# Leaving the masked quarter of each attention chunk out of two matrix products: 64x64 tiles in a one-core kernel of lightning attention and a tanh-shrink MLP

## The chip, the cores and the metric

The kernel runs on one core of a Trainium2 chip. The metric is the device time of one execution in microseconds (us); lower is better. Before the change three runs gave 674.28, 672.62 and 675.01 us, so the median is 674.28 us.

## The reference, cut to what matters

Two steps follow one another. The first is a causal linear attention with decay: for each of 4 batches and 8 heads (sequence 768, head width 64) the sequence is taken in blocks of 64. A block's output is a part inside the block plus a part from a 64x64 state that is carried along.

```python
rel = pos[:, None] - pos[None, :]                      # block = 64
Dmask = np.where(rel >= 0, lam[:, None, None] ** rel[None, :, :], 0.0)
for b in range(nb):                                    # 12 blocks
    intra = np.einsum('bhic,bhjc->bhij', qb, kb) * Dmask[None]
    intra = np.einsum('bhij,bhjd->bhid', intra, vb)
    inter = np.einsum('bhid,bhde->bhie', qb * lam_pow[None], kv_state)
    out[:, :, sl] = intra + inter
    kv_state = lam_block[None, :, None, None] * kv_state \
             + np.einsum('bhsd,bhse->bhde', kb * rev_pow[None], vb)
```

The result, seen as `x` of shape (3072, 512), then goes through

```python
h = x @ w_in            # 512 x 2048
g = h - np.tanh(h)
return g @ w_out        # 2048 x 512
```

The two weight matrices arrive as 64-bit floating point numbers and are rounded to 32 bit inside the kernel. All products are float32.

## The kernel before, in words

**Groups and halves.** The kernel takes the sequence in chunks of 128 (not 64), which is allowed because the state recurrence can be cut anywhere: inside a chunk the 128x128 lower triangle of the decay mask takes the place of the 64x64 one. There are six groups, g = 0 to 5; a group is one chunk of all four batches, 512 tokens. Attention of a group runs in two halves, batches 0 and 1 (called p0 in the driver) and batches 2 and 3 (p1). The eight heads are four pairs p = 0 to 3 with j = 0, 1 inside a pair.

**Attention of one half.** `att_transpose` brings q and k into the form "head width on partitions" (on TensorE for g = 0 and 1; for later groups the blocks of 32x32 come by many small loads, line 143, and VectorE transposes them). `att_scores` computes for each batch the scores `sp` = keys times queries, 128x128 per head, into two PSUM banks (line 351), and VectorE multiplies a bank of 512 columns with `mask` into `ss` (line 355). `att_out` gathers the half's output in two PSUM banks `op`: first state times decayed queries (line 399, 64x64 tiles of TensorE), then v times `ss` (line 405, 128x64 tiles, all 128 keys and all 128 queries); ScalarE copies the banks to `xt` (line 409). `att_state` decays the keys (line 360), multiplies them with v into `kv` (line 373), lets VectorE multiply `state` with `lam_blk` (line 378) and add `kv` (line 379). `att_sums` makes four sums of `xt` for the second step.

**The second step.** Both matrix products run as a two-by-two scheme with seven products instead of eight (in parts twice nested); its sums of weights are made once, written to DRAM, and come back piece by piece as `wb` on GpSimd's queue. TensorE lines 457 and 541 make h, line 740 h of group 0, lines 632, 685 and 769 the product with w_out. The sums of g for them (lines 619, 656, 669 to 671, 690, 695 to 701) are VectorE's.

**Order.** A scheduler keeps each engine's instructions in the order in which they are written where they are tied, and may move others by its own model of times. The driver lays the attention of group g+1 between the product steps of group g: `p0[0]` and `p0[1]` (transposes, scores) inside `up`, `p0[2:]` (output, state) after `down(g, 2)`, then `p1[0]`, `p1[1]` and `p1[2:]` between the `down_twice` steps. So between a half's scores and its output there are always other products on TensorE; and on VectorE a half's state update stands in one queue with the sums of g. For group 1 the same pieces lie between the steps of `up_plain` (line 740) and before `down_first` (line 769), while the weights are still being loaded and rounded.

**PSUM and loads.** `sp`, `op` and `kv` take turns in four banks. k, v and q come in "natural" form (sequence on partitions) by one load per batch and tensor on SyncE's queue (line 131), 256 KB each.

Of the kernel before, what the change touches and what calls it, by code (L numbers as in the profile page):

```python
# [9 lines left out]
F32 = mybir.dt.float32  # L10
# [5 lines left out]
AF = mybir.ActivationFunctionType  # L16
AL = mybir.AluOpType

BLK = 128
GB = 2  # L20
# [4 lines left out]
def kernel(  # L25
# [61 lines left out]
    dram = ctx.enter_context(tc.tile_pool(name="dram", bufs=1, space=bass.MemoryType.DRAM))  # L87


    ident = const.tile([128, 128], F32)  # L90
    make_identity(nc, ident)
    lam_all = const.tile([128, H], F32)
    nc.scalar.dma_start(out=lam_all, in_=bass.AP(tensor=lam.tensor, offset=lam.offset, ap=[[0, 128], [1, H]]))

    mask = const.tile([128, 2, NP, BLK], F32)
    for j in range(2):
        for p in range(NP):
            h = 2 * p + j
            nc.vector.tensor_tensor_scan(out=mask[:, j, p, :], data0=lam_all[:, h:h + 1].to_broadcast([128, BLK]),
                                         data1=ident, initial=0.0, op0=AL.mult, op1=AL.add)  # L100

    fwd = const.tile([128, NP, BLK], F32)

# [8 lines left out]
            m *= 2  # L112


    bwd = mask.rearrange("s j p i -> s p j i")[:, :, :, BLK - 1:BLK].to_broadcast([128, NP, 2, D])

    lam_blk = fwd[:, :, BLK - 1:BLK][:, None, :, :].to_broadcast([128, 2, NP, D])

    def tied(yes, op):
        return tc.keep_in_program_order(op) if yes else op  # L120


    raw, late = {}, {}
# [3 lines left out]
    def load_natural(g, b, names):  # L127
        for name, src, bufs in (("q", q, 2), ("k", k, 3), ("v", v, 4)):
            if name in names:
                x = (qpool if name == "q" else io).tile([128, H, D], F32, name=f"{name}_nat", tag=name, bufs=bufs)  # L130
                op = nc.sync.dma_start(out=x, in_=src[b, :, ts(g, BLK), :].rearrange("h s d -> s h d"))
                tc.keep_in_program_order(op)
                raw[g, b][name] = x

    def load_blocks(g, b, names):
# [86 lines left out]
    def weights(n):  # L222

        while ready["done"] < min(n, len(blocks)):
            at_ = ready["done"]
            load_weights(at_ + WAHEAD)
            kind, n_, m = blocks[at_]
            if kind == "out" and m == 0:
                pair[n_] = pair_tiles(n_)
            w = w1[n_][:, m] if kind == "in" else pair[n_][m][:, 0:2]  # L230
            if at_ in wraw:
                round_block(w, wraw.pop(at_), at_ < 2 * KI)
            else:
                load_block(nc.gpsimd, w, kind, n_, m)
            ready["done"] += 1
# [16 lines left out]
    def sums_out(kt):  # L252
        x, y = pair[kt]
        b11, b12, b21, b22, t1, t2, t4, t3 = (t[:, i] for t, n in ((x, 2), (y, 6)) for i in range(n))
        nc.vector.tensor_tensor(t1, b12, b11, op=AL.subtract)
        nc.vector.tensor_tensor(t2, b22, t1, op=AL.subtract)
        nc.vector.tensor_tensor(t3, b22, b12, op=AL.subtract)
        nc.vector.tensor_tensor(t4, b21, t2, op=AL.subtract)
        f = factors[:].rearrange("x p k c -> p x k c")
        nc.gpsimd.dma_start(out=f[:, 0:1, kt, :], in_=x[:, 0:1, :])  # L260
        nc.gpsimd.dma_start(out=f[:, 1:NX, kt, :], in_=y[:, 0:2, :])

        for n, j in ((1, 0),) if kt % 2 == 0 else ((2, 0), (3, 1)):
            nc.gpsimd.dma_start(out=fine[:, SUB.index(n), :, kt // 2, :].rearrange("n p c -> p n c"),
                                in_=y[:, 1:6, ts(j, 128)])
# [31 lines left out]
    def bank(name, tag, bufs):  # L297
        return psum.tile([128, 512], F32, name=name, tag=tag, bufs=bufs)
# [18 lines left out]
    state = const.tile([128, B, NP, D], F32)  # L317


    tr, sc, kdec, xt = {}, {}, {}, {}  # L320
# [23 lines left out]
    def att_scores(g, bs):  # L344
        for b in bs:
            qt, kt, _ = tr[g, b]

            sp = [bank("sp", "att", 4).rearrange("s (p i) -> s p i", p=NP) for _ in range(2)]
            for p in range(NP):
                for j in range(2):  # L350
                    tied(g == 0, nc.tensor.matmul(out=sp[j][:, p, :], lhsT=kt[ts(j, 64), p, :],  # L351
                                                  rhs=qt[ts(j, 64), p, :], start=True, stop=True))
            ss = work.tile([128, 2, NP, BLK], F32, name="ss", tag="ss")
            for j in range(2):
                tied(g == 0, nc.vector.tensor_tensor(ss[:, j], sp[j], mask[:, j], op=AL.mult))  # L355
            sc[g, b] = ss

    def att_decay(g, b):
        kp = raw[g, b]["k"].rearrange("s (p j) d -> s p j d", j=2)
        tied(g != 1, nc.vector.tensor_tensor(kp, kp, bwd, op=AL.mult))  # L360

    def att_state(g, bs):
        if g == NG - 1:
            return

        kv = bank("kv", "att", 4).rearrange("d (b p e) -> d b p e", b=2, p=NP)
        for n, b in enumerate(bs):
            kd, vn = raw[g, b]["k"], raw[g, b]["v"]
            if g > 0:
                att_decay(g, b)  # L370
            for p in range(NP):
                for j in range(2):
                    tied(g == 0, nc.tensor.matmul(out=kv[ts(j, 64), n, p, :], lhsT=kd[:, 2 * p + j, :],
                                                  rhs=vn[:, 2 * p + j, :], start=n == 0 and p == 0, stop=True,
                                                  skip_group_check=True))
        st = state[:, bs[0]:bs[0] + 2]
        if g > 0:
            nc.vector.tensor_tensor(st, st, lam_blk, op=AL.mult)
            nc.vector.tensor_tensor(st, st, kv, op=AL.add)
        else:  # L380
            tied(True, nc.scalar.activation(st, kv, AF.Copy))

    def att_out(g, bs):
        half = bs[0] // 2
        xt[g, half] = xpool.tile([128, KI, HB], F32, name=f"xt{half}", tag=f"xt{half}")

        ops = [bank("op", "att", 4).rearrange("d (p b s) -> d p b s", p=2, b=2) for _ in range(2)]

        def dst(n, p, j):
            return ops[p // 2][ts(j if p < 2 else 1 - j, 64), p % 2, n, :]  # L390


        if g > 0:
            for n, b in enumerate(bs):
                for p in (0, 1):
                    for j in range(2):
                        r = ts(j, 64)
                        for pp in (p, p + 2):
                            nc.tensor.matmul(out=dst(n, pp, j), lhsT=state[r, b, pp, :], rhs=tr[g, b][2][r, pp, :],  # L399
                                             start=n == 0 and p == 0, stop=False, skip_group_check=True)  # L400
        for n, b in enumerate(bs):
            ss, vn = sc.pop((g, b)), raw[g, b]["v"]
            for p in range(NP):
                for j in range(2):
                    tied(g == 0, nc.tensor.matmul(out=dst(n, p, j), lhsT=vn[:, 2 * p + j, :], rhs=ss[:, j, p, :],  # L405
                                                  start=g == 0 and n == 0 and p % 2 == 0,
                                                  stop=n == 1 and p % 2 == 1, skip_group_check=True))
        for x in range(2):
            tied(g == 0, nc.scalar.activation(
                xt[g, half][:, 2 * x:2 * x + 2, :].rearrange("d p (b s) -> d p b s", b=2), ops[x], AF.Copy))  # L410
# [9 lines left out]
        xt[g] = dict(B11=b11, B21=b21, B22=b22, T1=tt[:, 0], T2=tt[:, 1], T3=b12, T4=tt[:, 2])  # L420

    def attention(g):
        pieces = [[(fn, g, bs) for fn in (att_transpose, att_scores, att_out, att_state)] for bs in ((0, 1), (2, 3))]
        pieces[1].append((att_sums, g, None))
        return pieces

# [368 lines left out]
    def run(pieces):  # L795
        for fn, *args in pieces:
            fn(*args)


    for b in (0, 1):  # L800
# [31 lines left out]
    p0, p1 = attention(1)  # L832
    load(B + 2)
    turns = [(1, 11, 1, ()), (1, 21, 1, ()), (1, 12, 1, ()), (1, 22, 1, ()), (2, 11, 2, p0[0:1]), (2, 21, 2, p0[1:2]),
             (3, 11, 1, ()), (3, 21, 1, p0[2:4]), (2, 12, 1, ()), (2, 22, 1, p1[0:1]), (3, 12, 1, p1[1:2]),
             (3, 22, 1, ())]
    for u, c, n, more in turns:
        every(up_plain(u, (c,)))
# [8 lines left out]
            if u == 2:  # L847
                sums_in(0)
    sums_out(0)
    run(p1[2:4])  # L850
    weights(NU * KI + 6)
    run(p1[4:])
    for kt in range(KH):
        down_first(kt, (1, 2))
        if kt + 1 < KH:
# [99 lines left out]
```

## Time and profile before

| what | value |
|---|---|
| runs | 674.28, 672.62, 675.01 us (median 674.28) |
| profiled execution: span, first to last instruction | 670.7 us |
| around the span, by the median | 3.6 us |
| clock granted to TensorE | 1.00 in every stage |
| TensorE busy, share of the span | 654.7 us, 98% |
| VectorE busy | 477.8 us, 71% |
| ScalarE busy | 215.2 us, 32% |
| GpSimd busy | 199.0 us, 30% |
| `sp` products, line 351 (records, mean) | 384 records, 279 ns |
| `op` from state, line 399 | 320 records, 276 ns |
| `op` from `ss`, line 405 | 384 records, 275 ns |
| `kv`, line 373 | 320 records, 223 ns |

The profiled execution's time is known only as its span; what lies around it is taken as the 3.6 us by which the median is longer. A float32 product leaves two records in the trace, so 192 products of line 351 are 384 records. The mean of a record is its duration from fetch to end and says little on the pace, since records overlap; the pace is read from the distance of their starts. Of the 670.7 us some 57 at the start are ruled by the loading of w_in (the DMA engines are busy 96% of them), the next 76 by a chain of rounding, sums and DRAM round trips, and from 133 us on TensorE is busy nearly without a gap.

### The profile page before, as it was taken

The numbers are of one execution on the slowest core, as the hardware profiler recorded it, in microseconds if no ns is written. First come the engines' busy times: TensorE is split into PE (matmuls) and PEld (weight loads), VectorE is DVE, ScalarE is ACT, GpSimd is POOL, SyncE is SP. The second block draws the span as 40 slices with busy tenths as digits, with TensorE's granted clock in tenths as the row PEclk, the third lists the DMA queues.
The fourth block names the chain that finished last, engine by engine and source line by source line (L and its number), as shares of the span: only waits on it lengthen the run. The fifth ranks groups of instructions, "written<-read, shape, count | busy, mean of one in ns | idle before, by whom it ended". The sixth has DMA issues, their size and how long they took to land.

```text
span 670.7 us, 13240 instructions
## 1 busy us (share of the span) xinstructions
PE 654.7 (98%) x4992; PEld 594.8 (89%) x4992; DVE 477.8 (71%) x869; ACT 215.2 (32%) x413; POOL 199.0 (30%) x346
## 2 busy tenths in 40 slices
PE   8899989999999999999999999999999999999998
PEld 7688878788888899988999988899988899988897
DVE  4467988966877985379896378888358978357753
ACT  4778924512321112342112243112333112334110
POOL 0001444773022435101345200254300244400251
DMA  9999964999235979544698741698830676610395
GB/s 210 225 207 256 303 206 146 321 264 264 56 81 127 261 220 290 129 85 107 170 293 250 190 79 45 156 291 245 247 72 5 159 244 205 223 46 1 110 297 174
DMA packets 161007, 121.76 MB, mean 182 GB/s; under 512 B 133872, under 2 KB 135024, under 8 KB 160944
## 3 DMA queue, kind: packets, MB, share of 16 engines
q0 software_dynamic: 27264, 89.41, 41.4%
q1 hardware_dynamic: 133536, 31.50, 24.1%
q8 instruction: 40, 0.66, 0.4%
q14 instruction: 23, 0.19, 0.1%
q10 hardware_dynamic: 144, 0.00, 0.0%
HBM read 100.67 MB, written 20.19 MB: 180 GB/s over the span
## 4 chain that ended last, share of the span: by engine, by line
PE 69%; issue 11%; DMA 7%; DVE 5%; ACT 3%; POOL 3%; SPq 2%; POOLq 0%; DVEq 0%; ACTq 0%
PE y L457 12%; PE y L685 12%; PE zw L685 9%; PE z L457 8%; PE y L541 4%; PE w L632 4%; PE y L632 4%; PE acc L769 3%; DMA raw<-in_moe_w_in_dram 3%; PE sp L351 2%; PE z L541 2%; PE op L405 2%; SPq L210 1%; DMA fine<-f 1%; PE op L399 1%
## 5 line engine op out<-in xcount | busy, mean ns | idle before, releaser
L597 POOL DMA_DIRECT2D wb<-fine x168 | 90.5, 539 | 138.2 <-PE y L685 61.8
L465 ACT ACTIVATE th<-g 128x512 f32<-128x512 f32 x76 | 47.6, 630 | 99.2 <-DVE g L470 34.2
L688 ACT ACTIVATE q<-y 128x128 f32<-128x128 f32 x96 | 26.6, 277 | 149.5 <-PE y L685 148.5
L600 POOL DMA_DIRECT2D wb<-factors x44 | 23.8, 542 | 170.1 <-PE y L632 127.8
L457 PE MATMUL y<-xt,w 128*128 128x256 f32 x320 | 73.5, 380 | 0.0
L457 PEld LDWEIGHTS y<-xt,w 128*128 128x128 f32 x320 | 59.9, 190 | 8.5 <-ACT g L545 0.9
L466 DVE TENSOR_TENSOR g<-g,th 128x512 f32<-128x512 f32 x76 | 52.1, 688 | 21.1 <-ACT th L465 21.0
L685 PE MATMUL y<-wb,g 128*128 128x128 f32 x456 | 60.6, 278 | 0.0
L740 PE MATMUL h<-xt,w 128*128 128x256 f32 x256 | 58.1, 383 | 2.1 <-DVE w L295 2.1
L740 PEld LDWEIGHTS h<-xt,w 128*128 128x128 f32 x256 | 47.7, 190 | 10.0 <-DVE w L295 2.6
L685 PEld LDWEIGHTS y<-wb,g 128*128 128x128 f32 x456 | 55.1, 192 | 1.3 <-issue 0.3
L685 PE MATMUL zw<-wb,g 128*128 128x128 f32 x304 | 40.3, 275 | 0.1
L457 PE MATMUL z<-tt,ws 128*128 128x256 f32 x160 | 38.1, 381 | 0.0
L457 PE MATMUL y<-tt,ws 128*128 128x256 f32 x160 | 37.8, 379 | 0.0
L457 PE MATMUL z<-xt,ws 128*128 128x256 f32 x160 | 37.8, 379 | 0.0
L685 PEld LDWEIGHTS zw<-wb,g 128*128 128x128 f32 x304 | 37.0, 192 | 0.3 <-DVE g L690 0.3
L632 PE MATMUL w<-wb,g 128*128 128x256 f32 x160 | 35.8, 382 | 0.0
L769 PE MATMUL acc<-wt,g 128*128 128x256 f32 x144 | 33.2, 381 | 2.4 <-DVE g L775 2.4
L632 PE MATMUL y<-wb,g 128*128 128x256 f32 x160 | 35.3, 379 | 0.0
L355 DVE TENSOR_TENSOR ss<-sp,mask 128x512 f32<-128x512 f32 x48 | 31.0, 682 | 5.8 <-PE sp L351 5.8
L457 PEld LDWEIGHTS z<-xt,ws 128*128 128x128 f32 x160 | 30.4, 190 | 4.1
L632 PEld LDWEIGHTS y<-wb,g 128*128 128x128 f32 x160 | 30.4, 190 | 4.1
(179 smaller groups left out, 1291.2 us busy)
## 6 DMA issues: line engine op xcount, KB each, us to landing
wb<-fine POOLq DMA_DIRECT2D x168, 256.0 KB, 4.0
wb<-factors POOLq DMA_DIRECT2D x44, 256.0 KB, 4.1
raw<-in_moe_w_out_dram POOLq DMA_DIRECT2D x16, 512.0 KB, 5.4
v_nat<-in_v_dram SPq DMA_DIRECT2D x24, 256.0 KB, 4.9
wb<-fine_in POOLq DMA_DIRECT2D x24, 256.0 KB, 4.4
k_nat<-in_k_dram SPq DMA_DIRECT2D x20, 256.0 KB, 4.9
raw<-in_moe_w_in_dram SPq DMA_DIRECT2D x8, 512.0 KB, 6.2
raw<-in_moe_w_in_dram SPq DMA_DIRECT2D x16, 256.0 KB, 6.2
```

The source lines that it names most:

```text
L355: tied(g == 0, nc.vector.tensor_tensor(ss[:, j], sp[j], mask[:, j], op=AL.mult))
L457: nc.tensor.matmul(out=t[:, m, :], lhsT=wt[:, kt, ts(m, 128)], rhs=x[:, kt, :], start=first and m == 0 and kt == 0, stop=kt == 1, skip_gro ...
L465: nc.scalar.activation(th, src, AF.Tanh)
L466: nc.vector.tensor_tensor(dst(c), src, th, op=AL.subtract)
L541: nc.tensor.matmul(out=dst[:, ts(u, 128)], lhsT=a, rhs=b, start=x in (1, 2, 5) and u == 0, stop=True, skip_group_check=True)
L597: nc.gpsimd.dma_start(out=t.rearrange("p m c -> p (m c)"), in_=fine[TWICE.index(n_), SUB.index(x_)].rearrange("p u c -> p (u c)"))
L600: nc.gpsimd.dma_start(out=t, in_=factors[XAT[FACT[n_][1]]][:, 2 * x_:2 * x_ + 2, :])
L632: nc.tensor.matmul(out=t[:, m, :], lhsT=a[:, u, kt, ts(m, 128)], rhs=wb[:, kt, :], start=first and u == 0 and m == 0 and kt == 0, stop=u = ...
L685: nc.tensor.matmul(out=dst, lhsT=a[:, u, :], rhs=wb[:, ts(u, 128)], start=x in (1, 2) and u == 0, stop=u == NU - 1, skip_group_check=True)
L688: nc.scalar.activation(keep, dst, AF.Copy)
L740: tied(u == 0, nc.tensor.matmul(out=hm[c][:, m, :], lhsT=w1[u][:, i, a, ts(m, 128)], rhs=xt[0, t][:, i, :], start=m == 0 and i == 0, stop= ...
L769: nc.tensor.matmul(out=acc[n][:, r, :], lhsT=a[:, ts(r, 128)], rhs=b, start=kt == 0 and r == 0, stop=kt == KH - 1, skip_group_check=True)
```

## The change

Of a chunk's 128x128 scores (key by query) the quarter with keys 64 to 127 and queries 0 to 63 is masked to zero as a whole. The change leaves that quarter out of both products with 64-row blocks, and packs the other three.

- `mask` keeps three quarters per head: 6 blocks of 64 columns per j instead of 4 of 128. It is made from the whole mask by two further VectorE copies and an addition; `ident` gets 64 more columns.
- k and v are loaded so that heads 4 to 7 have their sequence halves exchanged (keys 64 to 127 on partitions 0 to 63). Each such load is three DMAs instead of one: heads 0 to 3 whole, heads 4 to 7 in two halves of partitions.
- `att_scores`: per head one product of keys 0 to 63 with all 128 queries, and one of keys 64 to 127 with queries 64 to 127, both in 64x64 tiles; per half 32 products instead of 16. The multiplication with the mask takes 384 columns instead of 512.
- `att_out`: for queries 64 to 127 one product per head with all keys (128x64 tile, 64 columns); for queries 0 to 63 one with keys 0 to 63 (64x64 tile, 64 columns). The `kv` products now stand between these two sets, and the keys are decayed before.
- The multiplication of `state` with `lam_blk` moves into `att_out`, is written for group 5 as well, and every product of the last set waits for it by an explicit dependency.
- `att_state` remains for group 0 alone; a half has three pieces instead of four.

```diff
-    mask = const.tile([128, 2, NP, BLK], F32)
+    nc.vector.tensor_copy(wide[:, 128:192], wide[:, 0:64])
+    mask = const.tile([128, 2, 6, HALF], F32)
...
+    nc.vector.tensor_copy(mask[:, :, 2:6, :], whole[:, :, :, HALF:BLK])
+    nc.vector.tensor_tensor(mask[:, :, 0:2, :], whole[:, :, 0:2, 0:HALF], whole[:, :, 2:4, 0:HALF], op=AL.add)
...
-                op = nc.sync.dma_start(out=x, in_=src[b, :, ts(g, BLK), :].rearrange("h s d -> s h d"))
-                tc.keep_in_program_order(op)
+                rows = src[b, :, ts(g, BLK), :].rearrange("h s d -> s h d")
+                if name == "q":
+                    parts = [(x, rows)]
+                else:
+                    parts = [(x[:, 0:4], rows[:, 0:4])] + [(x[ts(1 - t, HALF), 4:8], rows[ts(t, HALF), 4:8])
+                                                           for t in range(2)]
+                for to, of in parts:
+                    tc.keep_in_program_order(nc.sync.dma_start(out=to, in_=of))
...
-            for p in range(NP):
+            for p in (0, 2, 1, 3):
+                x, r = p % 2, p // 2
                 for j in range(2):
-                    tied(g == 0, nc.tensor.matmul(out=sp[j][:, p, :], lhsT=kt[ts(j, 64), p, :],
-                                                  rhs=qt[ts(j, 64), p, :], start=True, stop=True))
+                    kj, qj = kt[ts(j, 64), p, :], qt[ts(j, 64), p, :]
+                    k0, k1 = (kj[:, ts(t if r == 0 or g >= GB else 1 - t, HALF)] for t in range(2))
+                    tied(g == 0, nc.tensor.matmul(out=sp[j][ts(r, HALF), x:3 + p:2 + p - x, :], lhsT=k0,
+                                                  rhs=qj.rearrange("d (t i) -> d t i", t=2), start=True, stop=True))
+                    tied(g == 0, nc.tensor.matmul(out=sp[j][ts(1 - r, HALF), 2 + p, :], lhsT=k1,
+                                                  rhs=qj[:, HALF:BLK], start=True, stop=True))
...
+            decayed = nc.vector.tensor_tensor(st, st, lam_blk, op=AL.mult)
+        for n, b in enumerate(bs):
+            ss, vn = sc[g, b], raw[g, b]["v"]
+            for p in range(NP):
+                for j in range(2):
+                    tied(g == 0, nc.tensor.matmul(out=dst(n, p, j)[:, HALF:BLK], lhsT=vn[:, 2 * p + j, :],
+                                                  rhs=ss[:, j, 2 + p, :], start=g == 0 and n == 0 and p % 2 == 0,
+                                                  stop=n == 1 and p % 2 == 1, skip_group_check=True))
+        kv = kv_products(g, bs) if 0 < g < NG - 1 else None
         for n, b in enumerate(bs):
             ss, vn = sc.pop((g, b)), raw[g, b]["v"]
-            for p in range(NP):
+            for x in range(2):
                 for j in range(2):
-                    tied(g == 0, nc.tensor.matmul(out=dst(n, p, j), lhsT=vn[:, 2 * p + j, :], rhs=ss[:, j, p, :],
-                                                  start=g == 0 and n == 0 and p % 2 == 0,
-                                                  stop=n == 1 and p % 2 == 1, skip_group_check=True))
+                    for p in (x, 2 + x):
+                        r = ts(p // 2, HALF)
+                        op = nc.tensor.matmul(out=dst(n, p, j)[:, 0:HALF], lhsT=vn[r, 2 * p + j, :],
+                                              rhs=ss[r, j, x, :], start=False, stop=n == 1 and x == 1,
+                                              skip_group_check=True)
+                        tied(g == 0, op)
+                        if decayed is not None:
+                            tc.add_manual_dep(op.ins, decayed.ins.name, mybir.DependencyInfo(
+                                mybir.DependencyClass.Sync, mybir.DependencyReason.DATA), reason="rows")
+        if kv is not None:
+            nc.vector.tensor_tensor(st, st, kv, op=AL.add)
```

In the changed kernel the products of line 351 are at lines 373 and 375, those of line 405 become lines 429 (queries 64 to 127) and 439 (queries 0 to 63), line 399 becomes 422, line 373 becomes 393, and the multiplication of the state, line 378, becomes line 424.

More of the change, by code (lines that the diff above doesn't have):

```diff
@@ L87 @@
     dram = ctx.enter_context(tc.tile_pool(name="dram", bufs=1, space=bass.MemoryType.DRAM))
-    ident = const.tile([128, 128], F32)
+    wide = const.tile([128, 192], F32, name="ident")
+    ident = wide[:, 0:128]
     make_identity(nc, ident)
@@ L93 @@
     nc.scalar.dma_start(out=lam_all, in_=bass.AP(tensor=lam.tensor, offset=lam.offset, ap=[[0, 128], [1, H]]))
-    mask = const.tile([128, 2, NP, BLK], F32)
+    HALF = BLK // 2
+    nc.vector.tensor_copy(wide[:, 128:192], wide[:, 0:64])
+    mask = const.tile([128, 2, 6, HALF], F32)
+    whole = xpool.tile([128, 3, 2, HB], F32, name="whole", tag="tt").rearrange("s a b c -> s (a b c)")[:, 0:2 * DM].rearrange(
+        "s (j p i) -> s j p i", j=2, p=NP)
     for j in range(2):
@@ L98 @@
             h = 2 * p + j
-            nc.vector.tensor_tensor_scan(out=mask[:, j, p, :], data0=lam_all[:, h:h + 1].to_broadcast([128, BLK]),
-                                         data1=ident, initial=0.0, op0=AL.mult, op1=AL.add)
+            nc.vector.tensor_tensor_scan(out=whole[:, j, p, :], data0=lam_all[:, h:h + 1].to_broadcast([128, BLK]),
+                                         data1=ident if p < 2 else wide[:, HALF:HALF + BLK], initial=0.0, op0=AL.mult,
+                                         op1=AL.add)
+    nc.vector.tensor_copy(mask[:, :, 2:6, :], whole[:, :, :, HALF:BLK])
+    nc.vector.tensor_tensor(mask[:, :, 0:2, :], whole[:, :, 0:2, 0:HALF], whole[:, :, 2:4, 0:HALF], op=AL.add)
     fwd = const.tile([128, NP, BLK], F32)
@@ L112, in powers @@
             m *= 2
-    bwd = mask.rearrange("s j p i -> s p j i")[:, :, :, BLK - 1:BLK].to_broadcast([128, NP, 2, D])
+    bwd = mask.rearrange("s j p i -> s p j i")[:, 2:6, :, HALF - 1:HALF].to_broadcast([128, NP, 2, D])
     lam_blk = fwd[:, :, BLK - 1:BLK][:, None, :, :].to_broadcast([128, 2, NP, D])
@@ L346, in att_scores @@
             qt, kt, _ = tr[g, b]
-            sp = [bank("sp", "att", 4).rearrange("s (p i) -> s p i", p=NP) for _ in range(2)]
-            for p in range(NP):
+            sp = [bank("sp", "att", 4)[:, 0:6 * HALF].rearrange("s (x i) -> s x i", x=6) for _ in range(2)]
+            for p in (0, 2, 1, 3):
+                x, r = p % 2, p // 2
                 for j in range(2):
-                    tied(g == 0, nc.tensor.matmul(out=sp[j][:, p, :], lhsT=kt[ts(j, 64), p, :],
-                                                  rhs=qt[ts(j, 64), p, :], start=True, stop=True))
-            ss = work.tile([128, 2, NP, BLK], F32, name="ss", tag="ss")
+                    kj, qj = kt[ts(j, 64), p, :], qt[ts(j, 64), p, :]
[4 more added lines that the diff above has]
+                                                  rhs=qj[:, HALF:BLK], start=True, stop=True))
+            ss = work.tile([128, 2, 6, HALF], F32, name="ss", tag="ss")
             for j in range(2):
@@ L360, in att_decay, with kv_products @@
         tied(g != 1, nc.vector.tensor_tensor(kp, kp, bwd, op=AL.mult))
-    def att_state(g, bs):
-        if g == NG - 1:
-            return
+    def kv_products(g, bs):
         kv = bank("kv", "att", 4).rearrange("d (b p e) -> d b p e", b=2, p=NP)
@@ L368, in att_state @@
             kd, vn = raw[g, b]["k"], raw[g, b]["v"]
-            if g > 0:
-                att_decay(g, b)
             for p in range(NP):
@@ L375, in att_state @@
                                                   skip_group_check=True))
[L376 to L381, printed above, removed]
+        return kv
+    def att_state(g, bs):
+        kv = kv_products(g, bs)
+        tied(True, nc.scalar.activation(state[:, bs[0]:bs[0] + 2], kv, AF.Copy))
     def att_out(g, bs):
@@ L385, in att_out @@
         xt[g, half] = xpool.tile([128, KI, HB], F32, name=f"xt{half}", tag=f"xt{half}")
+        st = state[:, bs[0]:bs[0] + 2]
         ops = [bank("op", "att", 4).rearrange("d (p b s) -> d p b s", p=2, b=2) for _ in range(2)]
@@ L390, in dst @@
             return ops[p // 2][ts(j if p < 2 else 1 - j, 64), p % 2, n, :]
+        decayed = None
         if g > 0:
+            if g < NG - 1:
+                for b in bs:
+                    att_decay(g, b)
             for n, b in enumerate(bs):
@@ L422, in attention @@
     def attention(g):
-        pieces = [[(fn, g, bs) for fn in (att_transpose, att_scores, att_out, att_state)] for bs in ((0, 1), (2, 3))]
+        pieces = [[(fn, g, bs) for fn in (att_transpose, att_scores, att_out)] for bs in ((0, 1), (2, 3))]
         pieces[1].append((att_sums, g, None))
@@ L834 @@
     turns = [(1, 11, 1, ()), (1, 21, 1, ()), (1, 12, 1, ()), (1, 22, 1, ()), (2, 11, 2, p0[0:1]), (2, 21, 2, p0[1:2]),
-             (3, 11, 1, ()), (3, 21, 1, p0[2:4]), (2, 12, 1, ()), (2, 22, 1, p1[0:1]), (3, 12, 1, p1[1:2]),
+             (3, 11, 1, ()), (3, 21, 1, p0[2:]), (2, 12, 1, ()), (2, 22, 1, p1[0:1]), (3, 12, 1, p1[1:2]),
              (3, 22, 1, ())]
@@ L849 @@
     sums_out(0)
-    run(p1[2:4])
+    run(p1[2:3])
     weights(NU * KI + 6)
-    run(p1[4:])
+    run(p1[3:])
     for kt in range(KH):
```

## The prediction

> **What bounds the kernel now.** I read the page's busy shares first, then the table of windows by stage, then the chain of waits, then the timelines of TensorE and VectorE around each half's attention.
>
> ```profile
> PE 654.7 (98%) x4992; PEld 594.8 (89%) x4992; DVE 477.8 (71%) x869; ACT 215.2 (32%) x413; POOL 199.0 (30%) x346
> 90.00:100.00 10.00, 7.25 (x88) 5.95 (x86) 10.00 (x17) 0.60 (x1) 2.91 (x4) 1.00 0.44 150
> 312.00:365.00 53.00, 53.00 (x574) 50.16 (x573) 45.82 (x82) 8.98 (x25) 21.64 (x40) 1.00 0.83 228
> 417.00:470.00 53.00, 53.00 (x575) 50.19 (x574) 45.75 (x81) 8.99 (x25) 21.72 (x40) 1.00 0.83 229
> ```
>
> A row of the windows gives stretch, length, then the busy time of PE, PEld, DVE, ACT and POOL, the clock, DMA share and GB/s. In the two 53 us stretches with a group's attention TensorE has no gap: each 0.1 us taken off it there shortens the kernel, and each new wait lengthens it. From 90 to 100 us it is the other way round: VectorE is full, TensorE waits. In the chain of waits a half of group 3 reads so (start, us, engine, work):
>
> ```profile
> 315.64 1.99 PE sp L351 x32
> 317.62 7.10 PE w L632 x32
> 324.73 1.03 PE op L399 x32
> 325.76 1.90 PE op L405 x32
> 327.66 0.93 PE kv L373 x32
> 328.59 1.09 PE y L685 x8
> 329.68 0.89 PE zw L685 x8
> ```
>
> And VectorE at that time, from its timeline:
>
> ```profile
> 326.75 0.68 DVE L656 TENSOR_TENSOR o<-q,w 128x512 f32<-128x512 f32 x1
> 327.34 1.28 DVE L619 TENSOR_TENSOR g<-g,g 128x512 f32<-128x512 f32 x2
> 328.55 0.68 DVE L378 TENSOR_TENSOR state<-state,fwd 128x512 f32<-128x512 f32 x1
> ```
>
> No idle time stands in brackets behind these rows: VectorE works off a queue, and the state's multiplication (L378) begins 3.8 us after L399 only because sums stand ahead of it. Today nobody on TensorE waits for it.
>
> **What the products gain.** The pace is the distance of record starts. In L351 two records of 128 columns start per 112 ns, in L405 two per 109, in L373 (64 columns) two per 58, and in L399 (64x64 tiles) four per 109 ns. A change of tile shape adds about 0.09 us of gap and makes the first round some 0.05 longer; the y row shows the whole, 1.09 us behind `kv` and 0.89 later.
>
> Scores: 32 products make 64 records, four at a time: 8 rounds of 128 columns and 8 of 64. With first round and exit 0.161 + 7 x 0.109 + 8 x 0.058 + 0.10 = 1.49 us against 1.99: -0.50. The 64-column round in four tiles isn't in the trace; its bounds are 58 ns (the `kv` row) and 109 (the L399 row). I take 58, since halving the columns halves the pace in the `kv` row.
>
> Output: L429 is 32 records of 64 columns, two at a time, 0.11 + 15 x 0.058 = 0.98 us, against 1.80 from start to start for L405. `kv` keeps its 0.93 and its tile shape. L439 is 32 records in four tiles, 0.11 + 7 x 0.058 + 0.10 = 0.62, behind one more change of shape. From L405's start to the end of the half it was 1.80 + 0.93 + 0.10 (exit) = 2.83, and becomes 0.98 + 0.93 + 0.10 + 0.62 = 2.63: -0.20 (in group 5, without `kv`, 1.90 becomes 1.69). Were 64 columns as slow as 128 in four tiles, L439 would be 1.03 and this part would cost 0.2 instead. A half gains 0.70 us.
>
> Eight halves (groups 2 to 5) lie where TensorE has no gap: 8 x 0.70 = 5.6 us. Against the span of 670.7 this would be 665.1 and, with the 3.6 us around it, 668.7.
>
> **What the new wait costs.** All of L439 waits for L424, the old L378. The order of instructions in the changed kernel puts L424 at the same place of VectorE's queue, behind the same sums. TensorE comes to L439 at T0 + 1.03 (L399) + 0.98 (L429) + 0.93 (`kv`) + 0.10 = T0 + 3.04, T0 being the start of L399; in group 5, without `kv`, at T0 + 2.10. L424 ends, with 0.05 for the signal, where L378 ends now. Both T0 and VectorE's queue come earlier by about the same: TensorE by 0.50 from the scores, VectorE by four `ss` of 384 instead of 512 columns, whose pitch is 0.60 at 512 and 0.34 at 256, so 0.47 at 384 and 0.52 for the four. The difference to T0 therefore stays:
>
> - p0: group 2, T0 217.53, L378 ends 221.91: 4.43, a stall of 1.39. Group 3, 324.66 and 329.23: 4.62, 1.58. Group 4, 429.59 and 434.16: 1.58. Group 5 has no L378; L424 would follow L619, which starts at 536.60 with T0 534.52, and end at 537.88: 3.41 less 2.10 is 1.31.
> - p1: here the queue is short (L699 and L701 wait for TensorE and ScalarE, then L378).
>
> ```profile
> 349.45 0.41 DVE L695 TENSOR_TENSOR q<-q,zw 128x256 f32<-128x256 f32 x1
> 351.15 1.29 DVE L701 TENSOR_TENSOR q<-q,q 128x512 f32<-128x512 f32 x2
> 352.36 0.68 DVE L378 TENSOR_TENSOR state<-state,fwd 128x512 f32<-128x512 f32 x1
> ```
>
> Group 3 p1 has T0 349.78 and L378's end at 353.04, 3.31 with the signal, a stall of 0.27; groups 2 and 4 are the same within 0.01. Group 5: L424 behind L701 would end at 561.78, T0 is 558.74: 3.09 less 2.10 is 0.99.
>
> Together 1.39 + 1.58 + 1.58 + 1.31 + 3 x 0.27 + 0.99 = 7.7 us. Queued behind the waiting product on TensorE is all its later work, the y and zw products and through them the sums that VectorE makes next. A wait of 1.5 us lets VectorE catch up, but before the next half it waits for TensorE anyway (0.59 us before L690 at 330.61), so nothing is paid back. Groups 2 to 5: 7.7 - 5.6 = +2.1.
>
> **Group 1, while weights are still made.** TensorE has gaps here:
>
> ```profile
> 97.26 0.43 PE L399 MATMUL op<-qd,state 64*64 64x128 f32 x2 [2.58 <-DVE ss L355]
> 107.13 3.72 PE L769 MATMUL acc<-wt,g 128*128 128x256 f32 x16 [0.82 <-DVE g L775]
> ```
>
> p0 has T0 72.67 and L378's end at 77.87: a stall of some 2.2 us, of which the gap of 2.58 at 97.26 takes most back. In p1 five instructions of VectorE stand between the last `ss` and L378, whose end is 5.7 us behind T0: a stall of 2.7 to 3.7. Behind it wait L769 and, by `xt`, the sums L416 to L419 and L775; the gaps of 0.82 at 107.13 and 1.54 at 133.13 take 2.4 of it. The shorter `ss` and scores bring about 1 us. Bounds -3 to +4; I take 0, the middle of what is given and what the gaps take.
>
> **Start and loads.** The mask's two copies and one addition are about 1 us of VectorE, beside loads: the first scores come at 7.98 and the DMA engines are 96% busy until 57 us. Cost 0, and 0.2 if uncovered. Each k or v load is three DMAs instead of one, 88 more on SyncE's queue at the same bytes. One takes 0.4 us of the queue where it isn't held back (0.37 at 148.64), about 1.1 where it is. At 154 us twelve more stand ahead of the 128 block loads of group 2, 5 us at worst, and the last blocks are needed at about 232; TensorE's gap of 1.42 us at 233.57 is a `wb` load's and stays. Bounds 0 to +3, and I take +0.3, as most loads lie far ahead of use. Group 0 has three shorter products and no wait: within 0.2, and its stage is ruled by loads.
>
> Sum: 670.7 + 2.1 + 0 + 0.3 = 673.1, plus 3.6 around it: 676.7 us. A difference under 0.3% (2.0 us) can't be told from no change.
>
> **The rivals.** *The wait is hidden (faster).* If the scheduled instructions run so that L424 ends before T0 + 3.04 (2.10 in group 5), the 5.6 us stay: 674.3 - 5.6, with up to -2 in group 1, gives 667 to 669. It needs VectorE to be 1.5 us earlier at p0 relative to TensorE. For it: a TensorE that is held at one half may leave VectorE's queue shorter at the next; one half of each group is just 0.27 from the edge. Against it: VectorE's rows from 317.7 to 329.2 have no gap to give.
>
> *Four tiles do not run side by side with mixed lengths (slower).* Two at a time, scores would take 16 x 0.109 + 16 x 0.058 + 0.15 = 2.82 and L439 1.08, so a half costs +1.1 instead of -0.70. Later T0 also eases p0's wait: stalls of about 3 in all. 8 x 1.1 + 3 = +12, 686. If only the 64-column round costs 109, scores are 1.90, L439 1.03, a half +0.1, and with the stalls +8.5: 683. Against: the 32 records of L399 in 1.03 us. The Trainium skill, "TensorE: Matmul & The Clock Gate", "Part 3: Packing small matmuls", says that matmuls start and end strictly in program order; a short product behind a long one on another tile would then have to wait for it, and the sum would be by that page nearer to 683. The trace shows it for no mixed pair, since L399's products are all alike.
>
> *Group 1's wait isn't taken back (slower).* VectorE is full from 89 to 107 us, so a delay of 4 us there reaches 133 us whole once it exceeds the 2.4 us of gaps: 676.7 + 4 is 681. Against: half of it is waiting for loads.
>
> *The change saves nothing.* That the quarter is still computed is out: the instruction order shows 64-column operands on every product. That the split loads cost more than 0.3 is in the range.
>
> **How the numbers follow.** The forecast's case has 0.44 (its own range 672.5 to 680), the hidden wait 0.28, tiles not side by side 0.12, group 1's wait 0.11, loads or another delay 0.05. Of the forecast's case about 0.2 lies within 0.3% of 674.3 and the rest above; the hidden wait is faster. Faster 0.28, same 0.2, slower 0.52. Leaving out the last tenth of both ends, the range is 667.5 to 684.
>
> **What would show it.** In the profile after: 64 records of scores in about 1.5 us; L429 about 1.0, L439 about 0.6; L439's idle time in brackets, 1.3 to 1.6 us at p0 of groups 2 to 4 and 0.3 at p1, released by DVE state L424. No such brackets, or below 0.3 at p0, means the hidden wait. Scores over 1.9 us mean tiles in turn. A stage 57 to 133 us longer by over 3 us is the third rival, and a stage up to 233 us with k_blk or q_blk as releaser the loads. Wrong altogether would be TensorE slower in products that the change doesn't touch.

## The result, and the profile after

The changed kernel takes 684.23 us (median of 4 runs, 683.21 to 686.69) where the kernel before takes 674.03 in the same series: a ratio of 1.0142, 95% interval 1.0108 to 1.0175. The profiled execution has a span of 682.2 us against 670.7, 11.5 us more. That is more than the 10.2 us between the medians. In the runs on record the time mostly exceeds the span by 1.8 us (1.7 to 3.7), so the 3.6 taken for the kernel before were probably too much, and its trace is of one of its faster executions. The forecast was 676.7, with a range of 667.5 to 684, at whose upper end the result lies. Slower was right; of the loss the forecast saw a quarter.

The page of the changed kernel, and its windows (stretch, length, busy time of PE, PEld, DVE, ACT, POOL, clock, DMA share, GB/s):

```profile
PE 651.3 (95%) x5760; PEld 590.4 (87%) x5760; DVE 474.0 (69%) x874; ACT 215.7 (32%) x413; POOL 199.0 (29%) x346
```

```profile
0.00:57.00 57.00, 48.52 (x498) 41.09 (x499) 27.51 (x54) 33.55 (x56) 0.69 (x6) 0.97 0.85 194
100.00:133.00 33.00, 28.28 (x205) 24.41 (x200) 25.56 (x58) 11.85 (x19) 18.05 (x27) 0.95 0.58 189
215.00:312.00 97.00, 92.84 (x938) 86.39 (x931) 67.42 (x123) 23.82 (x52) 28.69 (x51) 0.98 0.68 180
312.00:365.00 53.00, 51.34 (x661) 47.31 (x661) 46.13 (x79) 9.90 (x24) 16.86 (x31) 1.00 0.70 188
417.00:470.00 53.00, 51.34 (x659) 47.22 (x658) 46.03 (x79) 9.96 (x24) 16.74 (x31) 1.00 0.70 188
```

TensorE is 3.4 us less busy, as meant, and idle for longer: 682.2 - 651.3 = 30.9 us, against 16.0 before. The two stretches of 53 us that had no gap now have 1.66 each. And three stages show a clock under 1.00, which the kernel before shows in none of its profiled execution.

Where the time went can be read by taking the same untouched product in both traces and subtracting its starts. In us, with the kernel before's time of the product on the left:

| product starts, before | lateness after | what lies between |
|---|---|---|
| 30.9 | +3.2 | start, loads of group 0 |
| 134.1 | +6.2 | group 1 |
| 248.7 | +8.7 | group 2 |
| 353.6 | +9.1 | group 3 |
| 458.6 | +9.6 | group 4 |
| 563.0 | +10.5 | group 5 |
| 667.3 | +11.4 | tail |

Groups 3 to 5 add 1.8 us; start, group 1 and group 2 add 8.7, the tail 1.0. First half of group 3, TensorE's timeline (start, us, work, idle time before it and its releaser) and VectorE's:

```profile
332.82 1.10 PE L422 MATMUL op<-qd,state 64*64 64x128 f32 x32
333.86 1.15 PE L429 MATMUL op<-ss,v_nat 128*64 128x64 f32 x32
334.84 1.10 PE L393 MATMUL kv<-v_nat,k_nat 128*64 128x64 f32 x32
337.40 0.69 PE L439 MATMUL op<-ss,v_nat 64*64 64x64 f32 x32 [1.46 <-DVE state L424]
338.03 1.16 PE L727 MATMUL y<-wb,g 128*128 128x128 f32 x8
```

```profile
335.46 1.28 DVE L661 TENSOR_TENSOR g<-g,g 128x512 f32<-128x512 f32 x2
336.66 0.68 DVE L424 TENSOR_TENSOR state<-state,fwd 128x512 f32<-128x512 f32 x1
```

From start to start L429 is 0.98 us and L439 0.63. L439 waits for L424, and L424 for its turn behind the sums of L661: the stall that the forecast priced at 1.58 is 1.46 in brackets. The scores of this half, their first record and the product behind them:

```profile
324.22 0.32 PE L373 MATMUL sp<-qt,kt 64*64 64x128 f32 x1
...
325.72 7.17 PE L674 MATMUL w<-wb,g 128*128 128x256 f32 x32
```

That is 1.50 us where 1.99 were.

What the forecast had at 0 and 0.3 us is at the start and in group 2. SyncE's queue, the kernel before and then the changed one:

```profile
8.22 1.14 SPq L131 DMA_DIRECT2D k_nat<-in_k_dram  x1
9.40 1.77 SPq L207 DMA_DIRECT2D raw<-in_moe_w_in_dram  x2
```

```profile
10.39 1.88 SPq L150 DMA_DIRECT2D k_nat<-in_k_dram  x3
12.31 1.27 SPq L225 DMA_DIRECT2D raw<-in_moe_w_in_dram  x2
```

The first load of w_in is issued 2.9 us later, because a k or v load takes 1.9 us of the queue instead of 0.6 to 1.1 (once 1.8). The DMA engines themselves are less busy in the first 57 us than before, 85% against 96%. And the three longest gaps of the changed kernel on TensorE:

```profile
20.49 1.69 PE L782 MATMUL h<-xt,w 128*128 128x256 f32 x4 [2.05 <-DVE w L313]
...
106.08 1.08 PE L439 MATMUL op<-ss,v_nat 64*64 64x64 f32 x32 [4.32 <-DVE state L424]
...
241.90 1.35 PE L727 MATMUL zw<-wb,gS 128*128 128x128 f32 x8 [2.68 <-DVE gS L732]
```

The gap at 241.90 names L732, but VectorE was late for another reason:

```profile
239.96 0.71 DVE L348 STREAM_TRANSPOSE kt<-k_blk 128x512 f32<-128x512 f32 x1 [2.68 <-DMA k_blk<-in_k_dram]
...
241.17 0.68 DVE L732 TENSOR_TENSOR gS<-gS,s 128x512 f32<-128x512 f32 x1
```

A transpose waits 2.68 us for group 2's last block load, and the sum that TensorE needs stands behind it in VectorE's queue.

### The profile page after: what moved, and what is told of

It reads as the page before. It is cut to its first block, busy times and chain, and to the rows that moved or that the text cites. A ratio compares the mean times of both kernels' runs of the same rounds, so it can differ in the third digit from the quotient of the medians.

```text
span 682.2 us, 14924 instructions
## 1 busy us (share of the span) xinstructions
PE 651.3 (95%) x5760; PEld 590.4 (87%) x5760; DVE 474.0 (69%) x874; ACT 215.7 (32%) x413; POOL 199.0 (29%) x346
## 4 chain that ended last, share of the span: by engine, by line
PE 57%; issue 10%; SPq 10%; DVE 9%; DMA 8%; ACT 4%; POOL 2%; POOLq 0%; DVEq 0%; ACTq 0%
PE y L727 11%; PE y L499 10%; PE zw L727 8%; SPq L161 8%; PE z L499 6%; PE h L782 5%; PE acc L811 4%; PE y L583 4%; PE y L674 3%; SPq L150 2%; DMA q_blk<-in_q_dram 2%; PE z L583 2%; ACT r L309 1%; DVE g L661 1%; PE end L766 1%
## 5 line engine op out<-in xcount | busy, mean ns | idle before, releaser
L727 PE MATMUL y<-wb,g 128*128 128x128 f32 x456 | 60.6, 278 | 0.0
L727 PEld LDWEIGHTS y<-wb,g 128*128 128x128 f32 x456 | 55.1, 192 | 0.9
L727 PE MATMUL zw<-wb,g 128*128 128x128 f32 x304 | 40.2, 275 | 0.0
L727 PEld LDWEIGHTS zw<-wb,g 128*128 128x128 f32 x304 | 37.0, 192 | 0.0
L451 ACT ACTIVATE xt<-op 128x512 f32<-128x512 f32 x24 | 13.1, 602 | 70.6 <-PE op L439 70.6
L223 POOL DMA_DIRECT2D raw<-in_moe_w_out_dram x16 | 8.8, 549 | 87.7 <-ACT r L310 78.5
```

The source lines that it names most:

```text
L727: nc.tensor.matmul(out=dst, lhsT=a[:, u, :], rhs=wb[:, ts(u, 128)], start=x in (1, 2) and u == 0, stop=u == NU - 1, skip_group_check=True)
```

## The experiments

Two theories were open. A: the split loads cost most of what was missed, by SyncE's time per DMA. B: the wait of L439 does, above all in group 1. Each was taken away alone, then both, and A was put alone into the kernel before. Each series had its own runs of the kernel before (medians 675.0 to 676.6), so ratios are compared. Each ratio has an interval of some ±0.2 to 0.3%, so a difference of two ratios is good to some 2 to 3 us.

**Whole loads.** One DMA per k and v load again.

```diff
-                if name == "q":
+                if True:
                     parts = [(x, rows)]
```

> The changed kernel with one DMA per k and v load, as before; heads 4 to 7 then hold their halves unexchanged, so half of the output's values are not the reference's. Theory A (the split loads cost most of what the forecast missed: the first w_in load is issued 2.9 us later, at 12.31 instead of 9.40, and group 2's last block load lands late, a gap of 2.68 us at 241.90 and a halved clock behind it): some 3 us back at the start and 4 in group 2, so 677 to 678. Theory B (the wait of L439 in group 1 makes the rest): 682 to 684.

Measured: 677.43 us, ratio 1.0031 (1.0001 to 1.0062), so 1.1% or 7.5 us off the changed kernel's 1.0142. On the first series' scale (674.03) that is 676, with 674 to 678 as its interval: theory A's number within the noise, and not theory B's 682 to 684.

**L439 behind a one-column copy of ScalarE.** The explicit dependency keeps L439 behind L422; both write the same PSUM banks, from different row tiles. No run here leaves that order out, so the wait is given another releaser.

```diff
-            decayed = nc.vector.tensor_tensor(st, st, lam_blk, op=AL.mult)
+            spent = tr[g, bs[1]][2][:, NP - 1, 0:1]
+            decayed = nc.scalar.activation(spent, spent, AF.Copy)
+            nc.vector.tensor_tensor(st, st, lam_blk, op=AL.mult)
```

> The changed kernel, but L439 waits for a one-column ScalarE copy that overwrites a spent column of qd (so it still comes behind L422), instead of for the state's multiplication on VectorE; everything else as it was. Theory B (the wait itself): the stalls on L439 go, 6.9 us in groups 2 to 5 as the trace shows them (1.27 + 0.21 + two times about 1.5 and 0.3 + 1.2 + 0.8) and 1 to 4 in group 1: 673 to 676. Rival: VectorE's backlog is waited for at the next step anyway, in the y and zw products: over 680.

Measured: 677.11 us, ratio 1.0016 (0.9984 to 1.0048), 8.5 us off, or 675 on the first series' scale, as expected. The rival falls: VectorE's backlog isn't waited for again. The late blocks show more strongly here, since TensorE comes to them earlier: it waits 6.72 us for the same sum (there line 734).

**Both.**

> Both edits together (one DMA per load, heads 4 to 7 unexchanged, so half of the output's values are not the reference's; L439 behind the ScalarE copy). Theories A and B together: only the products' gain of 0.70 us per half is left, 5.6 us and about 1 in group 1: 667 to 669, the forecast's hidden wait. If the gain itself is smaller than costed, 671 to 674.

Measured: 670.13 us, ratio 0.9905 (0.9874 to 0.9936), 16 us off. The two edits add up (7.5 + 8.5), and what is left is a gain of 6.4 us. So within the noise the whole loss is these two costs, and the products do gain what they were costed at. By stage, what the trace of each version loses against that of the kernel before (single executions; up to 134.1, 248.7, 563.0 and 667.3 us of its time):

| version | start, group 1 | group 2 | groups 3 to 5 | tail |
|---|---|---|---|---|
| the change | 6.2 | 2.5 | 1.8 | 1.0 |
| whole loads | 2.6 | -0.2 | 1.8 | 1.0 |
| ScalarE copy | 3.7 | 6.5 | -3.9 | 0.9 |
| both | 0.5 | 0.7 | -3.2 | 1.2 |

The loads cost 3.2 to 3.6 us up to 134.1 and 2.7 to 5.8 in group 2; the wait costs 2.1 to 2.5 up to 134.1 and 5.1 to 5.7 in groups 3 to 5. Theory B's "above all in group 1" falls.

**The split loads alone, in the kernel before.**

```diff
-                op = nc.sync.dma_start(out=x, in_=src[b, :, ts(g, BLK), :].rearrange("h s d -> s h d"))
+                parts = [(x[:, 0:4], rows[:, 0:4])] + [(x[ts(t, 64), 4:8], rows[ts(t, 64), 4:8])
+                                                       for t in range(2)]
```

> The kernel before with each k and v load in three DMAs (heads 0 to 3, and heads 4 to 7 in two halves of partitions, put where they were), nothing else. Theory A: 3 us at the start and 2.5 to 4 in group 2: 679 to 681. The forecast's term (+0.3): 674 to 675.

Measured: 681.39 us, ratio 1.0073 (1.0045 to 1.0102): 5 us, 679 on the first series' scale. That this is less than the 7.5 of the changed kernel is within the noise of the two differences. In its trace 2.6 us are lost by 31 us and 5.0 by 134. In group 2 the gap at 233.57, which the kernel before spends on a `wb` load, takes 1.9 back, and one of 1.43 us on the late transposes gives 1.6 again (4.7 at 249). Another 2.8 of that trace come in groups 3 and 4, 1.30 and 1.08 of it as gaps before L691 with `wb` loads as releaser, and 0.6 in the tail; theory A doesn't explain these.

**Other places for the loads.** With the copy in place of the wait, k and v of groups 0 and 1 were put on GpSimd's queue; then group 2's first loads too; then the state's multiplication on ScalarE; then group 2's first loads behind the blocks of their batch. In the texts below "the first" is the first of these four versions.

```diff
-                    tc.keep_in_program_order(nc.sync.dma_start(out=to, in_=of))
+                    tc.keep_in_program_order((nc.gpsimd if name != "q" and g < GB else nc.sync).dma_start(out=to, in_=of))
```

> The changed kernel with L439 behind the ScalarE copy, and with the k and v loads of groups 0 and 1 (three DMAs each) issued on GpSimd's queue, which has nothing to do in the first 57 us; q and w_in stay on SyncE, groups 2 to 5 as in the change. Theory A (SyncE's time per DMA is the price, not the smaller transfers): the 3 us at the start come back and group 2's 4 to 9 stay, so 2 to 4 us under the version with the copy alone, a ratio of 0.995 to 0.999 to the kernel before. Rival (the transfers in halves themselves are slower): no gain, 1.0016 again.

> As the one before, and the first k and v loads of group 2 (batches 0 to 2), which stand ahead of its 128 block loads, on GpSimd's queue too. Theory A: group 2's blocks start about 8 us earlier on SyncE than in the change, the late transposes go, and with them the halved clock: a ratio of 0.988 to 0.992, the same as with whole loads. Rival: GpSimd's queue holds them up behind wb loads that wait for their buffers, and v or k is late: over 0.995.

Measured: ratios of 1.0165 (1.0137 to 1.0192) and 1.0075 (1.0053 to 1.0096). Theory A's numbers failed in both: the start isn't mended but worse. By 57 us of the kernel before's time the first is 6.9 us late where the version with the copy alone was 4.3, by 134.1 it is 8.2 against 3.7. One large piece of it is the copy itself:

```profile
86.48 1.13 PE L441 MATMUL op<-ss,v_nat 64*64 64x64 f32 x32 [5.29 <-ACT qd L425]
```

ScalarE rounds weights in this stage, and the copy waits for its turn there as L424 did on VectorE. How the rest divides between transfers that now come before w_in and a changed order on the engines wasn't separated, so these runs don't decide between theory A and its rival, smaller transfers that are slower themselves. What speaks for theory A is that SyncE issues the w_in load late and that the DMA engines are less busy meanwhile. Group 2's gap does go with the second (9.8 us late at 243, 10.3 at 233.6), as theory A wants.

```diff
-            decayed = nc.vector.tensor_tensor(st, st, lam_blk, op=AL.mult)
+            for p in range(NP):
+                decayed = nc.scalar.activation(st[:, :, p, :], st[:, :, p, :], AF.Copy, scale=fwd[:, p, BLK - 1:BLK])
```

> As the first of this call, but the multiplication of the state is done by ScalarE itself (four activations of 128 columns with a scale per partition), and L439 waits for these instead of for the one-column copy; VectorE has ten operations of 0.60 us less. If ScalarE's queue is free there: four times some 0.28 us end 1.1 us behind L399, before L439's turn 2.0 us behind it, so no wait, and the same as the first within 2 us. If ScalarE is held up by other activations, waits of up to 1 us per half come back: 3 to 6 us slower.

Measured: 1.0161 (1.0140 to 1.0182), the same as the first. Ten operations less on VectorE are worth nothing in this version.

```diff
-            for b in first:
-                load_natural(g, b, nat)
             for b in range(B - 1):
                 load_blocks(g, b, "qk")
+                if b in first and b:
+                    for c in (0, 1) if b == 1 else (2,):
+                        load_natural(g, c, nat)
```

> As the first of this call, but on SyncE the first k and v loads of group 2 come behind the block loads of the batch that they belong to, not ahead of all. Theory A: the blocks of batches 0 and 1 start 8 to 10 us earlier, but the last block load, behind all, is as late as before (it waits for the same number of DMAs), so the gap in group 2 stays unless the queue had slack: 0 to 4 us under the first.

Measured: 1.0067 (1.0050 to 1.0084), 6.6 us better than the first, more than expected: lateness grows by 1.3 us from 233.6 to 243, not by 6.4. The expectation was wrong in its reason: as many DMAs stand ahead of the last block, but the queue no longer stands still in front of them. The last experiment shows it on SyncE's rows. The wait for the copy in group 1 stays, 6.24 us in this version's trace.

**The copy, and group 2's loads behind its blocks, all on SyncE.**

> The changed kernel with L439 behind the ScalarE copy and, on SyncE, the first k and v loads of group 2 behind the block loads of the batch that they belong to; all loads on SyncE. If group 2's late blocks are what the copy alone left (9 us between 233.57 and 242.97 of the kernel before's time, of which the version with late loads on GpSimd lost 1.3): 7 to 8 us under the copy alone, a ratio of 0.990 to 0.994. Rival: the 3.7 us that it had lost by 134 us grow, and the gain of groups 2 to 5 is eaten: 0.997 to 1.000.

Measured: 671.09 us, ratio 0.9946 (0.9923 to 0.9968). With both repairs the packing is faster than the kernel before, with all loads split in three.

**Packing only where TensorE is the bound.** Groups 0 and 1 as before the change, groups 2 to 5 packed with both repairs. The main lines, against the changed kernel:

```diff
+    def att_scores(g, bs):
+        if g >= GB:
+            return scores_packed(g, bs)
...
+    def att_out(g, bs):
+        if g >= GB:
+            return out_packed(g, bs)
...
-                if name == "q":
+                if g < GB:
```

> Groups 0 and 1 as in the kernel before (whole loads, 128x128 scores, no exchanged halves), groups 2 to 5 as in the change, with the ScalarE copy and the late loads of the version beside it; the packed mask is made from the whole one behind group 1, 9 operations of VectorE. Theory: TensorE isn't the bound before 133 us, so packing gains nothing there and its loads and waits only cost; without them 0 is lost up to 134 us, then 8 halves gain 0.70 each, 5.6, less 1 to 2 in group 2: 670 where the kernel before takes 674, a ratio of 0.991 to 0.995, the same as or up to 4 us under the version beside it. Rival: making the packed mask delays a sum at 133 us, or weights (wb) that now come too late for a faster TensorE take the gain: 0.997 to 1.000.

Measured: 669.66 us, ratio 0.9912 (0.9894 to 0.9930): 6 us faster than the kernel before. In its trace 1.0 us is lost by 134 us, then 5.0 gained up to 563. The first half of group 3 reads

```profile
323.20 1.10 PE L467 MATMUL op<-qd,state 64*64 64x128 f32 x32
324.23 1.15 PE L476 MATMUL op<-ss,v_nat 128*64 128x64 f32 x32
325.21 1.10 PE L442 MATMUL kv<-v_nat,k_nat 128*64 128x64 f32 x32
326.25 0.69 PE L486 MATMUL op<-ss,v_nat 64*64 64x64 f32 x32
326.87 1.16 PE L805 MATMUL y<-wb,g 128*128 128x128 f32 x8
```

with no bracket: L486 begins 3.05 us behind the state products, and the half's output takes 3.67 us from start to start, where it took 3.86.

**Each cost again, in that version.** First L439's wait on VectorE put back, then the loads ahead of the blocks put back.

```diff
-            spent = tr[g, bs[1]][2][:, NP - 1, 0:1]
-            decayed = nc.scalar.activation(spent, spent, AF.Copy)
-            nc.vector.tensor_tensor(st, st, lam_blk, op=AL.mult)
+            decayed = nc.vector.tensor_tensor(st, st, lam_blk, op=AL.mult)
```

> Groups 0 and 1 as before the change, groups 2 to 5 packed with the late loads, and L439 waiting for the state's multiplication on VectorE as in the change. This is the forecast's own case without group 1 and the loads: stalls of 7.7 us by the forecast's list against the version with the ScalarE copy (0.9912), so 7 to 8 us more, a ratio of 1.001 to 1.003. If the stalls were mostly group 1's doing and the later halves hide them: 0.992 to 0.996.

Measured: 1.0017 (0.9989 to 1.0045), so 1.05% or 7.1 us (give or take 2) for the wait in groups 2 to 5. The forecast's list came to 7.7.

> Groups 0 and 1 as before the change, groups 2 to 5 packed with the ScalarE copy, and group 2's first k and v loads ahead of its block loads as in the change (fifteen DMAs instead of five at about 0.6 us of SyncE each). Theory A: the last blocks land some 4 to 5 us late, a stall of 3 to 9 us at 234 to 243 us with a halved clock: 0.995 to 1.003. Rival: without the delay of the first stages there is slack for it: 0.990 to 0.994.

Measured: 1.0002 (0.9977 to 1.0026), 6.1 us (give or take 2) for the order of six k and v loads, five of which come behind the stop shown below. TensorE and VectorE in that run:

```profile
240.77 2.08 PE L804 MATMUL zw<-wb,gS 128*128 128x128 f32 x8 [5.45 <-DVE gS L809]
```

```profile
238.83 0.71 DVE L359 STREAM_TRANSPOSE kt<-k_blk 128x512 f32<-128x512 f32 x1 [4.36 <-DMA k_nat<-in_k_dram]
```

The profile names the k_nat load that stands next to the block in SyncE's queue; a transpose of `k_blk` needs the block, so I read this wait as the block's too. SyncE's rows in this run, and then with the blocks first:

```profile
126.80 1.93 SPq L161 DMA_DIRECT2D k_nat<-in_k_dram  x3
151.35 1.74 SPq L161 DMA_DIRECT2D v_nat<-in_v_dram  x3
...
161.29 13.22 SPq L172 DMA_DIRECT2D q_blk<-in_q_dram  x16
```

```profile
139.82 11.46 SPq L172 DMA_DIRECT2D q_blk<-in_q_dram  x16
```

With the loads first the queue stands still from 128.7 to 151.35 ahead of a v load; with the blocks first the block loads begin at 139.82, 21 us earlier, and the last block load ends at 226.95 instead of 233.61. The same stop is in the kernel before (from 124 to 148.6); there the blocks were still just in time. As what the k and v loads waited for, the table of the queue's waits names `fine<-f`, the writing of the sums of weights to DRAM (72.4 us in three waits, with the loads first). A releaser is inferred, and no run tested this one.

## Why the prediction was right or wrong

**The step that failed: the price of the split loads.** The sum had +0.3 us for them. Taking them away gives 7.5 us back, and alone in the kernel before they cost 5. The issue time was read about right: each additional DMA took 0.3 us of the queue at the start and 0.5 in group 2. What failed is that it would be covered by work ahead of it, at both places (below). Slower was forecast for another reason, a wait that costs more than the products gain, priced at 2.1 us. That term came: the version with just that (groups 2 to 5 packed, the wait put back) loses 2.3 us in its trace from 134 to 563 us, though its ratio, 1.0017, can't be told from 1. But it is small against noise, so that slower came out this clearly is luck. So is it that the result lies at the range's end: that end comes in part from tiles that don't run side by side, which did not happen.

**The products' gain, right.** 0.70 us per half was forecast: 0.50 from the scores, 0.20 from the output. Measured, the scores of a half gain 0.49 (1.50 for 1.99, in seven of the eight halves; the eighth lies in a stretch of half the clock), and the output, in the version without the wait, 0.19. That pieces of 128 and 64 columns run side by side in four tiles, which no row showed, is shown now: 64 records in 1.50 us; two at a time would have been 2.8. So the rival of tiles in turn is out, though its 683 to 686 is where the time came to lie. The rule quoted there from the Trainium skill ("TensorE: Matmul & The Clock Gate", "Part 3: Packing small matmuls"), that matmuls start and end in program order, costs nothing here by these 1.50 us. The order of p lets each tile get one long and one short product per pair, which may be why; whether the products end in order no run shows, since the ends of records are modelled.

**The wait in groups 2 to 5, right.** Stalls of 7.7 forecast, 7.1 by the run that puts the wait back. In the traces the outputs of the eight halves are 7.5 us longer in the changed kernel than in the version that packs the late groups with the copy, 1.3 to 1.5 at p0 of groups 2 to 4 and 0.3 at p1, and 1.3 and 1.0 in group 5. Groups 3 to 5 were to lose 0.45 + 0.45 + 0.9 = 1.8 us by their terms and lose 1.8.

**Group 1, wrong by its size.** The term was 0, with bounds of -3 and +4. Its wait is 4.32 us in the second half and 1.11 in the first; the version with the copy alone is 1.5 us late at 101.7 where the change is 5.4 late, so the wait costs 3.9 there, and 2.1 to 2.5 are left of it at 134.1 (the table above). In the trace with whole loads the second half has no such wait, so the 4.32 comes from the loads and the wait together. The forecast let the gaps at 97.26, 107.13 and 133.13 take most of it back. The first two are gone from the changed kernel's trace, as forecast. The last, of 1.54, is still there, because what it waits for is later by the same amount. A gap ahead takes up a delay only if its releaser isn't delayed with it.

**The start, wrong.** It stood at 0 together with the mask, with the split loads at +0.3 in all and +3 as a bound. The 88 DMAs of 0.4 us each were let count for 0.3 us in all, "as most loads lie far ahead of use". The k and v loads do, but the w_in load behind them in the same queue doesn't: the first product of w_in is 2.5 us late and, by 31 us, 3.2.

**Group 2, wrong.** The term was weighed correctly (5 us at worst, last blocks needed at 232) and then set at 0.3. The queue resumes at 153.65 instead of 148.64, since all before it is late, five loads then take 10.8 us instead of 5.6, and the last block load ends at 235.34 instead of 225.09, 10.3 us later, where TensorE was 6 late. The change loses 2.68 us at the gap and 1.7 behind it by the clock (below), of which 2.5 are left with the waits on L424, the products' gain and the `wb` gap at 233.57, which isn't there any more. 6.1 us are lost by the run that puts the order back alone: the place of these loads ahead of the blocks, where single DMAs were still just in time, is what costs.

**The tail, not seen.** 1.0 us: L727 waits 0.79 us for a `wb` load at 653.91. The version with both edits loses 1.2 there too. It is less than what single executions differ by.

Of the 11.5 us of the two spans, 1.8 were forecast for groups 3 to 5 and came; the start and group 1 make 6.2, group 2 makes 2.5, the tail 1.0.

## What to carry to other kernels

A wait costs what is queued ahead of its releaser: the same ordering of L439 behind L422 cost 7 us by VectorE's queue and nothing by a one-column copy on a ScalarE that was free there, while that same copy was waited for 5.3 us where ScalarE was full. A load split in three took about two to three times as long to issue here (1.9 us against 0.6 to 1.1), and the bill went to whoever stood behind it, w_in and the block loads, not to the tensor that was split. Apply a packing only in the stages whose bound it relieves: with both repairs 1.4% slower became 0.5% faster, and 0.9% with groups 2 to 5 packed alone, a step at the edge of the noise.

## What the runs showed of the hardware that was not expected

A gap on TensorE has a second price. Behind the three gaps shown above the granted clock falls to half for about 3.4 us; at the third one, by windows of 1 us (the clock is the third number from the end):

```profile
242.00:243.00 1.00, 1.00 (x8) 1.00 (x9) 0.97 (x2) 0.00 (x0) 0.00 (x0) 0.87 1.13 289
243.00:244.00 1.00, 1.00 (x7) 1.00 (x6) 0.82 (x3) 0.00 (x0) 0.45 (x1) 0.50 1.05 235
...
246.00:247.00 1.00, 1.00 (x47) 0.93 (x39) 0.59 (x2) 0.00 (x0) 0.00 (x0) 0.93 0.72 136
```

It begins 0.1 to 0.8 us after work has resumed. The products from the gap at 241.90 up to 246.96 take 5.06 us; before, the same took 3.87, of which the scores' gain should have taken 0.49. So the slow stretch costs 1.7 us, half of its 3.4. Gaps of 2.05, 2.68 and 4.32 us did it, the kernel before's of 2.58 at 97.26 did not. So the length of a gap alone doesn't tell. The two versions that pack groups 2 to 5 with late loads, with the copy and with the wait, have the same gap of 2.89 us at the same product:

```profile
97.74 0.43 PE L519 MATMUL op<-qd,state 64*64 64x128 f32 x2 [2.89 <-DVE ss L407]
...
99.42 0.43 PE L517 MATMUL op<-qd,state 64*64 64x128 f32 x2 [2.89 <-DVE ss L407]
```

Behind the first the clock is 0.50 from 99.0 to 102.4, behind the second it stays at 1.00. The Trainium skill ("TensorE: Matmul & The Clock Gate", "Part 1: The HAM clock gate") has a clock of one half after an idle window of some 3.4 us, counted in windows that run freely. The half and the length of the slow stretch agree; here gaps shorter than 3.4 us sufficed.

Executions of one and the same kernel differ in this too: the ten of the version with whole loads have mean clocks from 1.000 (674.89 and 675.01 us) to 0.990 (683.10 us), and of the 26 of the kernel before in that series only six have 1.000, down to 0.994. So one trace's clock is not the kernel's. No run held the gaps and took away the clock's fall, so its share of the 10 us is an estimate: three times 1.7, at most 5 us.
